# Loading q, k and v as nine consecutive tokens per partition, with the reordering done on the chip

## The chip, the cores and the metric

The kernel runs on one core of one Trainium2 chip. The time is the device time of one execution in microseconds (us), quoted as the median of several runs. Engines are named as in the profile: PE is the tensor engine (PEld its weight loads), DVE the Vector engine, ACT the Scalar engine, POOL is GpSimd (here it mostly issues loads), SP issues the stores. A ratio of two kernels is the mean time of one kernel's runs over that of the other's in the same rounds, so it is not quite the ratio of the medians that stand beside it. Executions over 1.5% slower than the fastest of the same kernel are left out of the means.

## The reference

Sliding-window causal attention (64 tokens back, batch 8, 8 heads, 576 tokens, head size 64), whose output is the input of a soft mixture of experts with 32 slots.

```python
def _attn_ref(q, k, v):                      # (8, 8, 576, 64)
    scores = scale * np.matmul(q, k.transpose(0, 1, 3, 2))
    mask = (rel >= 0) & (rel < 64)
    # ... softmax over the masked scores, then attn @ v

def _moe_ref(x, phi, w1, w2):                # x (4608, 512), 8 experts of 4 slots
    logits = x @ phi
    d = softmax(logits, over tokens); c = softmax(logits, over slots)   # shortened
    slot_input = (d.T @ x).reshape(8, 4, 512)
    for e in range(8):
        slot_out[e] = np.maximum(slot_input[e] @ w1[e], 0.0) @ w2[e]
    return c @ slot_out
```

The inputs are 28.3 MB of q, k, v and 33.5 MB of expert weights in fp32. The loads cast them to fp16, so 14.2 and 16.8 MB are written on the chip. The output is 9.4 MB.

## The kernel before

Each partition holds one token of a 128-token chunk, all heads beside each other. Every contiguous run in memory is one head's 64 numbers, 256 bytes. There are buffers for only five experts' weights, and `v_shf`, a copy of V moved by 64 tokens, is made by a transfer within the on-chip memory.

```python
for t_bf, t_dram in ((q_bf, q), (k_bf, k)):
    for c in range(NC):                                  # 5 chunks of tokens
        # ...
        nc.gpsimd.dma_start(out=t_bf[0:pn, c],
            in_=t_dram[b, :, 128 * c: 128 * c + pn, :].rearrange("h p d -> p h d"))
# ... the same for v_aug, then two transfers v_shf <- v_aug

def stage_tr(b, hp, q_bf, k_bf, small):                  # transposes: plain matmul with identity
    # ...
    for c in range(4):
        nc.tensor.matmul(tq[:, 128 * c:128 * c + 128], q_bf[:, c, h0:h0 + 2, :],
                         ident_h[:, :], start=True, stop=True)
    nc.scalar.copy(out=qT[:, 0:512], in_=tq[:, :])       # unit stride on both sides
    # ... k the same, its copy on DVE

    if b >= B - 5:
        load_expert(b - (B - 5))                         # five of the eight experts
```

The softmax here doesn't subtract the row's maximum and nothing guards it: scores larger than these inputs give would overflow.

## Time and profile before

The median was 295.81 us (293.19 to 296.01, 3 runs) before the prediction, and 294.73 us (4 runs) in the rounds of the comparison.

| stage, by the first matmul of the next | from, us | to, us | what bounds it |
|---|---|---|---|
| attention and the MoE's front | 0 | 216 | the 16 DMA queues, and waits for v_shf |
| experts | 216 | 260 | three experts' weights that come late |
| output | 260 | 291 | the stores |

From the page of the kernel before: its span, then the busy tenths of the DMA engines in 40 equal slices (7.3 us each), what they moved, and the sizes of the packets.

```profile
span 291.3 us, 5506 instructions
DMA  7999999999999999999999999900006999909997
GB/s 42 138 114 184 106 165 142 161 216 162 114 182 188 116 208 205 143 143 188 146 140 208 176 128 170 207 6 2 0 0 102 186 210 211 160 0 318 348 362 268
DMA packets 135338, 45.62 MB, mean 157 GB/s; under 512 B 113808, under 2 KB 126096, under 8 KB 135312
```

The engines read as busy in nearly every slice up to 190 us, but move 106 to 216 GB/s: most packets are small. Then they idle while GpSimd waits for a free weight buffer. From the list of waits of the kernel before (who waited for whom: us in total, times, longest):

```profile
POOL w1s L87 <- PE hj L276: 46.8, 2, 46.3
PE av L146 <- DMA v_shf<-v_aug: 37.8, 9, 9.1
```

The groups by line and shape give the durations (busy us, mean ns of one):

```profile
L112 DVE CAST kT<-tk 128x512 f16<-128x512 f32 x32 | 21.7, 679 | 13.2 <-PE tk L109 12.7
L106 ACT CAST qT<-tq 128x512 f16<-128x512 f32 x32 | 19.5, 610 | 9.3 <-PE tq L103 9.3
L127 DVE TENSOR_TENSOR pmt<-pmt,mask_95 128x256 f16<-128x256 f16 x64 | 18.5, 289 | 13.0 <-ACT pmt L126 12.2
```

A copy of 512 elements out of the matmul's result memory (PSUM) takes 0.61 us on ACT and 0.68 us on DVE.

### The profile page before, as it was taken

The page shows a single profiled execution, that of the slowest core. Times are in us where ns is not written, and L with a number is a line of the kernel's source. Part 1 is how long each engine was busy: PE and PEld are TensorE (multiplying, and loading weights), DVE is VectorE, ACT ScalarE, POOL GpSimd, SP SyncE. Part 2 cuts the span into 40 slices and gives each one's busy share as a digit, 9 for nine tenths or more (in the row PEclk, how much of TensorE's full clock was granted, in tenths as well). Part 3 has the DMA queues.
Part 4 walks back from the last instruction along what each step waited for, and adds up shares of the span by engine and source line. Part 5 has one row for each costly group of instructions (what it writes and reads, how often), then busy time and mean ns, then how long its engine had stood idle before and what let it go on. Part 6 is the DMA issues. An engine that isn't in the chain of part 4 may idle for free.

```text
span 291.3 us, 5506 instructions
## 1 busy us (share of the span) xinstructions
PE 200.2 (69%) x2080; PEld 114.1 (39%) x2080; DVE 126.2 (43%) x459; ACT 123.7 (42%) x403; POOL 116.1 (40%) x148
## 2 busy tenths in 40 slices
PE   0231858757983974996786598598878996685850
PEld 0120745544562552654454456354433432221100
DVE  1030871971682594378189068357320000023331
ACT  1030555553463653635465345464502332144552
POOL 9999396255486471838636380000003300000000
PEclk9999999955555885555596555575669999596555
DMA  7999999999999999999999999900006999909997
GB/s 42 138 114 184 106 165 142 161 216 162 114 182 188 116 208 205 143 143 188 146 140 208 176 128 170 207 6 2 0 0 102 186 210 211 160 0 318 348 362 268
DMA packets 135338, 45.62 MB, mean 157 GB/s; under 512 B 113808, under 2 KB 126096, under 8 KB 135312
## 3 DMA queue, kind: packets, MB, share of 16 engines
q0 software_dynamic: 125584, 30.97, 145.4%
q1 hardware_dynamic: 9728, 14.31, 16.5%
q8 instruction: 16, 0.26, 0.4%
q14 instruction: 10, 0.08, 0.1%
HBM read 61.93 MB, written 9.44 MB: 245 GB/s over the span
## 4 chain that ended last, share of the span: by engine, by line
DMA 29%; PE 22%; issue 20%; POOL 12%; DVE 7%; ACT 7%; ACTq 0%; DVEq 0%; SPq 0%; POOLq 0%
DMA v_shf<-v_aug 14%; DMA w1s<-in_moe_w_dram 7%; DMA out_dram<-ob 5%; POOL v_aug L219 4%; PE tx L164 4%; DMA v_aug<-in_v_dram 3%; PE av L146 3%; PE ltA L173 3%; POOL k_bf L212 3%; POOL q_bf L212 3%; ACT ob L303 3%; PE sA L122 2%; PE dps L198 2%; DVE kT L112 2%; ACT pmt L128 1%
## 5 line engine op out<-in xcount | busy, mean ns | idle before, releaser
L146 PE MATMUL av<-v_shf,pmt 128*64 128x65 f16 x320 | 30.9, 239 | 41.1 <-DMA v_shf<-v_aug 37.8
L212 POOL DMA_DIRECT2D q_bf<-in_q_dram x40 | 33.7, 873 | 32.1 <-PE tq L103 15.2
L126 ACT ACTIVATE pmt<-sA 128x256 f16<-128x256 f32 x64 | 24.8, 388 | 48.9 <-PE small L122 37.9
L212 POOL DMA_DIRECT2D k_bf<-in_k_dram x40 | 34.0, 874 | 21.2 <-DMA w2s<-in_moe_w_dram 12.4
L146 PEld LDWEIGHTS <-pmt 128*64 128x64 f16 x576 | 22.3, 140 | 50.3 <-issue 30.4
L219 POOL DMA_DIRECT2D v_aug<-in_v_dram x40 | 33.7, 871 | 8.0 <-DMA k_bf<-in_k_dram 2.6
L122 PEld LDWEIGHTS <-kT 64*128 64x128 f16 x576 | 23.6, 113 | 22.6 <-issue 10.8
L167 ACT CAST xT<-tx 128x512 f16<-128x512 f32 x32 | 18.1, 591 | 31.6 <-PE tx L164 31.6
L122 PE MATMUL sA<-qT,kT 64*128 64x64 f16 x512 | 25.9, 223 | 6.5 <-DVE kT L112 6.5
L146 PE MATMUL av<-v_aug,pmt 128*64 128x65 f16 x256 | 29.2, 241 | 0.0
L151 DVE RECIPROCAL rc<-av 128x5 f32<-128x5 f32 x64 | 9.6, 176 | 44.5 <-PE av L148 44.1
L152 DVE TENSOR_TENSOR x_b<-av,rc 128x320 f16<-128x320 f32 x64 | 28.2, 479 | 0.1
L112 DVE CAST kT<-tk 128x512 f16<-128x512 f32 x32 | 21.7, 679 | 13.2 <-PE tk L109 12.7
L128 ACT ACTIVATE pmt<-sA 128x256 f16<-128x256 f32 x64 | 25.0, 390 | 0.0
L87 POOL DMA_DIRECT2D w1s<-in_moe_w_dram x8 | 6.1, 768 | 47.1 <-PE hj L276 46.8
L306 DVE TENSOR_SCALAR ob<-cps,crcp 128x512 f32<-128x512 f32 x16 | 11.2, 745 | 29.9 <-PE cps L301 17.9
L127 DVE TENSOR_TENSOR pmt<-pmt,mask_95 128x256 f16<-128x256 f16 x64 | 18.5, 289 | 13.0 <-ACT pmt L126 12.2
L109 PE MATMUL tk<-ident_h,k_bf 128*128 128x128 f16 x128 | 22.5, 281 | 2.1 <-DMA k_bf<-in_k_dram 2.1
L276 PE MATMUL hj<-w1s,slot_inT 128*4 128x512 f16 x64 | 19.8, 428 | 5.9 <-DMA w1s<-in_moe_w_dram 5.5
L106 ACT CAST qT<-tq 128x512 f16<-128x512 f32 x32 | 19.5, 610 | 9.3 <-PE tq L103 9.3
L130 DVE TENSOR_TENSOR pmt<-pmt,mask_95 128x320 f16<-128x320 f16 x64 | 20.7, 323 | 3.6 <-ACT qT L105 0.3
L301 PE MATMUL cps<-slot_oa,dnumT 32*128 32x512 f16 (+1 forms) x40 | 15.9, 508 | 7.4 <-ACT ob L303 6.7
(72 smaller groups left out, 345.9 us busy)
## 6 DMA issues: line engine op xcount, KB each, us to landing
w1s<-in_moe_w_dram POOLq DMA_DIRECT2D x8, 1024.0 KB, 12.6
w2s<-in_moe_w_dram POOLq DMA_DIRECT2D x8, 1024.0 KB, 17.0
out_dram<-ob SPq DMA_DIRECT2D x8, 1024.0 KB, 4.5
q_bf<-in_q_dram POOLq DMA_DIRECT2D x32, 128.0 KB, 6.8
k_bf<-in_k_dram POOLq DMA_DIRECT2D x32, 128.0 KB, 8.0
v_aug<-in_v_dram POOLq DMA_DIRECT2D x32, 128.0 KB, 8.3
v_shf<-v_aug SPq DMA_DIRECT2D x8, 330.0 KB, 6.7
v_shf<-v_aug SPq DMA_DIRECT2D x8, 264.0 KB, 8.2
```

What stands on the lines that cost most here:

```text
L106: nc.scalar.copy(out=qT[:, 0:512], in_=tq[:, :])
L109: nc.tensor.matmul(tk[:, 128 * c:128 * c + 128], k_bf[:, c, h0:h0 + 2, :], ident_h[:, :], start=True, stop=True)
L112: nc.vector.tensor_copy(out=kT[:, 64:576], in_=tk[:, :])
L122: nc.tensor.matmul(dst, kT[r0:r0 + 64, 64 * i: 64 * i + 128], qT[r0:r0 + 64, 64 * i: 64 * i + 64], start=True, stop=True)
L126: nc.scalar.activation(pmt[:, 0:4, :], sA[:, 0:4, :], AF.Exp, scale=scale)
L128: nc.scalar.activation(pmt[:, 4:8, :], sA[:, 4:8, :], AF.Exp, scale=scale)
L130: nc.vector.tensor_tensor(out=pmt[:, 4:9, :], in0=pmt[:, 4:9, :], in1=mask_bB, op=ALU.mult)
L146: nc.tensor.matmul(av[r0b: r0b + 64, 65 * (i // 2): 65 * (i // 2) + 65], pmt[:, i, :], rhs, start=True, stop=True)
L152: nc.vector.tensor_tensor(out=x_b[:, 0:NC, 64 * h: 64 * h + 64], in0=avv[:, 0:NC, 1:65], in1=rc[:, 0:NC].unsqueeze(2).broadcast_to([128, N ...
L212: nc.gpsimd.dma_start(out=t_bf[0:pn, c], in_=t_dram[b, :, 128 * c: 128 * c + pn, :].rearrange("h p d -> p h d"))
L219: nc.gpsimd.dma_start(out=v_aug[0:pn, :, c, 1:65], in_=v[b, :, 128 * c: 128 * c + pn, :].rearrange("h p d -> p h d"))
L276: nc.tensor.matmul(hj[0:SPE, :], slot_inT[:, dc, SPE * e: SPE * e + SPE], w1s[:, dc, 512 * j: 512 * j + 512], start=(dc == 0), stop=(dc == ...
```

## The change

The intent is large runs and no second trip. One partition gets nine consecutive tokens of one head, 2304 contiguous bytes. After the transposes on PE the tokens stand in the wrong order (all tokens 0, 9, 18, ... first), and the copy out of PSUM puts them right by writing at a stride of nine elements. v_shf disappears; V is transposed a second time into windows instead. All weights are loaded during attention, and the expert and output stages use all of PE's columns. Work proceeds in 16 half batches of four heads.

```diff
-                nc.gpsimd.dma_start(
-                    out=t_bf[0:pn, c],
-                    in_=t_dram[b, :, 128 * c: 128 * c + pn, :].rearrange("h p d -> p h d"))
+            t = pld.tile([128, 2, S], FP16, name=nm, tag=nm)
+            nc.gpsimd.dma_start(
+                out=t,
+                in_=src[b, 4 * half:4 * half + 4].rearrange(
+                    "(x h) (g t) d -> (h g) x (t d)", x=2, h=2, t=T))      # T = 9
...
+    def t1(src, dst, on_vector):
+        for t0, n in ((0, 5), (5, 4)):
+            tr = ps.tile([128, 8, 128], FP16, name="tr", tag="tr")         # two buffers in all
+            for j in range(n):
+                for x in range(2):
+                    nc.tensor.transpose(tr[64 * x:64 * x + 64, j, :],
+                                        src[:, x, 64 * (t0 + j):64 * (t0 + j) + 64], ident[:, :])
+            o = dst.rearrange("p h (g t) -> p t h g", t=T)[:, t0:t0 + n]
+            i = tr[:, 0:n, :].rearrange("p t (h g) -> p t h g", h=2)
+            if on_vector:
+                nc.vector.tensor_copy(out=o, in_=i)
+            else:
+                nc.scalar.copy(out=o, in_=i)
...
+    def issue_loads(u):
+        if u + 2 < nu:
+            load_unit(u + 2)
+        for _ in range(1 if u >= 1 else 0):
+            if w_order and len(w_order) > 3:
+                f, e = w_order.pop(0)                                       # one w1 or w2
+                f(e)
```

The `tr` buffers serve the first transposes of q, k, v, the second of V, and all of the MoE front.

## The prediction

> **What bounds it now.** Span 291.3 us. The table by windows shows three stages. (1) 0–210 us, attention with the MoE front: the DMA row reads 9 in nearly every slice until 185 us, at only 140–185 GB/s of bytes written; of 135,338 packets 113,808 are under 512 B (q, k, v in 64-token runs), and v_shf, an SBUF copy that each batch waits for, stands in the chain of waits with 14%. PE is busy 75–80%. (2) 210–259 us, experts: only five experts' weights fit; GpSimd's next weight load waits 46.3 us for PE's hj, DMA is idle 190–220 us, then three experts (6.3 MB) arrive in 30 us, at 207 GB/s. (3) 259–291 us, output, 9.4 MB at 310–360 GB/s.
>
> **What the change does.** q, k, v: 2304 B contiguous per descriptor, 48 loads instead of 120, no v_shf (4.75 MB). All weights load during attention. In return 3 q/k/v reorder passes per half batch: per half batch ("unit", 16 of them) about 174 matmuls, in total 3,030 against 2,080.
>
> Costs per unit, estimates from the trace's durations:
> - DMA: 14.2+16.8 MB at 207 GB/s = 150 us in all; 0.885 MB of q/k/v is 4.3 us, a weight 5.1 us. In GpSimd's order the 16th unit's loads come after nearly all weights: six middle units carry two weights each, 14.4 us per unit; the last four carry none. The eleventh-to-twelfth unit arrives near 132 us.
> - PE: 128-column matmuls start 107 ns apart at clock 0.5, 56 ns at 1.0; 64-column ones in pairs about 55 ns a pair. At half clock 2.9 us first transposes, 1.9 us V transposes, 2.2 us QK/AV, 2 us MoE: 9.1 us. The Trainium skill, "TensorE: Matmul & The Clock Gate", Part 4, says transpose mode does not count as busy for the clock; before used plain matmuls, so its trace cannot tell. I expect mostly 0.5 here.
> - DVE: mask 2.1, V copies 2.0, k 1.5, normalise 2.3, MoE 1.2: 9.1 us, taking 0.53 ns per element (as the mask shows) for 16-bit PSUM copies with unit step; the skill, "VectorE: DVE Perf Modes", perf-mode tier table, allows up to 2x there. Otherwise 11.
> - ACT 5.4 us.
>
> With waits between the in-order engines (two shared transpose banks, one AV buffer) I take 10.5–12 us per unit where compute binds.
>
> **Sum.** To 132 us the DMA binds; then 5.3 units × 11 us = 58 and 8 us for the last batch's MoE: attention ends near 198. Experts, no weight waits, 22 us (PE, four column groups at once, near clock 1.0): 220. Output 31: 251, and 3 more outside the profile's span: **254 us**, range **236 to 274**. Faster by over 2%: 0.94; within 2%: 0.04; slower: 0.02. So about 40 us: some 27 from the expert stage, 12 from attention, 1–2 from output.
>
> **What would show it.** Right: no v_shf, few packets under 512 B, DMA about 200 GB/s until about 150 us and idle after; PE and DVE dense (over 85%) from 135 to 195 at clock about 0.5; experts under 26 us without DMA waits; output DMA-bound near 350 GB/s. Wrong: DMA below 180 GB/s in attention (2304 B runs not efficient); DVE's V copy of 512 elements near 0.68 us instead of 0.41; experts at clock 0.5 (34 us).
>
> **What would make it wrong.** Waits between PE, ACT and DVE making a unit 14 us or more, so that compute binds all 16 units (over 280); or full clock and short waits (8 us per unit), giving about 236.

## The result

The changed kernel takes 416.17 us (median, 415.28 to 416.71, 4 runs) against 294.73 us: a ratio of 1.4104 (95% interval 1.4025 to 1.4184). It is 41% slower, where 254 us was expected. The result is correct.

The page of the changed kernel (slices of 10.4 us):

```profile
span 414.8 us, 6919 instructions
PE 208.4 (50%) x3028; PEld 152.7 (37%) x3028; DVE 204.5 (49%) x420; ACT 221.8 (53%) x160; POOL 51.7 (12%) x77
DMA  8993997969693979596423324240003300000798
GB/s 110 191 180 49 137 153 105 184 84 184 89 187 48 188 124 177 89 173 112 58 28 43 46 30 57 30 54 5 1 2 53 50 2 2 2 0 2 287 377 246
DMA packets 31069, 40.83 MB, mean 98 GB/s; under 512 B 1856, under 2 KB 22336, under 8 KB 31040
```

What the change was meant to do to the DMA, it did: 31,069 packets instead of 135,338, and hardly any below 512 bytes. But no engine is busy for more than 53% of the span, and the DMA is idle for nearly half of it. Attention ends at 361 us (before: 216). The experts then take 23 us (before: 44) and the output 31 (before: 32).

Groups by line and shape of the changed kernel:

```profile
L143 ACT COPY qT<-tr 128x640 f16<-128x640 f16 x16 | 47.5, 2971 | 15.2 <-PE tr L136 15.2
L143 ACT COPY qT<-tr 128x512 f16<-128x512 f16 x16 | 40.0, 2497 | 0.0
L141 DVE COPY kT_111<-tr 128x512 f16<-128x512 f16 x8 | 20.9, 2616 | 0.0
L169 DVE COPY vw_113<-tr 128x512 f16<-128x512 f16 x32 | 12.2, 417 | 30.0 <-PE tr L167 30.0
L191 DVE TENSOR_TENSOR pm<-pm,mask_98 128x512 f16<-128x512 f16 x64 | 24.4, 418 | 15.7 <-ACT pm L187 15.6
```

The copies after the first transposes (lines 141 and 143) take 2.5 to 3.0 us on both engines. The copy of V into windows (line 169) has the same 512 fp16 elements from the same PSUM buffers on the same engine and takes 0.417 us. The one difference in plain sight is where the elements are written. Three such pairs of copies stand in every half batch: 5.2 us for k on DVE and 10.6 us for q and v on ACT ((85.5 + 42.0 + 41.9) / 16, from the page's rows of line 143).

What follows from that shows in the order of time. From the timeline of the changed kernel (start us, us, what, and in brackets how long the engine had been idle and what ended it):

```profile
156.52 1.01 PE L167 MATMUL tr<-ident,vT_103 128*128 128x128 f16 x8 [1.24 <-ACT qT L143]
158.58 5.21 DVE L141 COPY kT_111<-tr 128x640 f16<-128x640 f16 x2 [0.25 <-PE tr L136]
161.59 1.01 PE L249 MATMUL tr<-ident,x_bp 128*128 128x128 f16 x8 [2.52 <-DVE kT_111 L141]
163.84 0.37 PE L167 MATMUL tr<-ident,vT_103 128*128 128x128 f16 x2 [1.24 <-DVE rc L220]
165.57 5.23 ACT L143 COPY vT_112<-tr 128x640 f16<-128x640 f16 x2 [6.45 <-PE tr L136]
170.86 1.03 PE L167 MATMUL tr<-ident,vT_112 128*128 128x128 f16 x8 [3.72 <-ACT vT_112 L143]
```

A pair of copies (the two that empty one tensor's transposes) holds both `tr` buffers, and PE, whose next work in order is a transpose into one of them, stands still (2.5 and 3.7 us here). So the slow copies on the two engines do not overlap with each other but follow one another. GpSimd's next load waits for PE in turn. From the waits:

```profile
POOL qn L61 <- PE tr L136: 74.7, 12, 8.9
POOL vn L61 <- PE av L214: 70.7, 11, 8.6
PE tr L167 <- ACT qT L143: 25.5, 15, 2.1
PE tr L167 <- ACT vT_112 L143: 20.8, 8, 3.7
```

A half batch takes 21.9 us: the first transposes of v run from 13.2 us (half batch 0) to 342.3 us (half batch 15), which is 329.1 / 15.

### The profile page after: what moved, and what is told of

The parts are those of the page before. It is cut to its first block, busy times and chain, and to the rows that moved or that the text cites. A ratio compares the mean times of both kernels' runs of the same rounds, so it can differ in the third digit from the quotient of the medians.

```text
span 414.8 us, 6919 instructions
## 1 busy us (share of the span) xinstructions
PE 208.4 (50%) x3028; PEld 152.7 (37%) x3028; DVE 204.5 (49%) x420; ACT 221.8 (53%) x160; POOL 51.7 (12%) x77
## 2 busy tenths in 40 slices
DMA packets 31069, 40.83 MB, mean 98 GB/s; under 512 B 1856, under 2 KB 22336, under 8 KB 31040
## 5 line engine op out<-in xcount | busy, mean ns | idle before, releaser
L143 ACT COPY qT<-tr 128x640 f16<-128x640 f16 (+1 forms) x32 | 85.5, 2734 | 15.2 <-PE tr L136 15.2
L143 ACT COPY vT_112<-tr 128x640 f16<-128x640 f16 (+1 forms) x16 | 42.0, 2845 | 52.4 <-PE tr L136 52.4
L143 ACT COPY vT_103<-tr 128x640 f16<-128x640 f16 (+1 forms) x16 | 41.9, 2832 | 44.5 <-PE tr L136 44.5
L187 ACT ACTIVATE pm<-sc 128x1024 f16<-128x1024 f32 (+1 forms) x48 | 46.4, 967 | 33.0 <-issue 28.1
L141 DVE COPY kT_102<-tr 128x640 f16<-128x640 f16 (+1 forms) x16 | 41.7, 2794 | 9.9 <-PE tr L136 9.9
L141 DVE COPY kT_111<-tr 128x640 f16<-128x640 f16 (+1 forms) x16 | 41.7, 2790 | 2.2 <-PE tr L136 2.2
L167 PE MATMUL tr<-ident,vT_112 128*128 128x128 f16 x144 | 19.4, 307 | 45.6 <-ACT vT_112 L143 20.8
L169 DVE COPY vw_104<-tr 128x512 f16<-128x512 f16 (+1 forms) x48 | 15.0, 353 | 47.9 <-PE tr L167 47.9
L167 PE MATMUL tr<-ident,vT_103 128*128 128x128 f16 x144 | 19.9, 306 | 37.1 <-ACT vT_103 L143 13.4
L191 DVE TENSOR_TENSOR pm<-pm,mask_98 128x512 f16<-128x512 f16 (+1 forms) x96 | 29.8, 349 | 15.7 <-ACT pm L187 15.6
L167 PEld LDWEIGHTS <-vT_112 128*128 128x128 f16 x144 | 14.4, 135 | 48.0 <-issue 25.0
L169 DVE COPY vw_113<-tr 128x512 f16<-128x512 f16 (+1 forms) x48 | 15.2, 352 | 30.0 <-PE tr L167 30.0
L214 PEld LDWEIGHTS <-pm 128*64 128x64 f16 x576 | 28.1, 158 | 4.7 <-issue 2.4
L167 PEld LDWEIGHTS <-vT_103 128*128 128x128 f16 x144 | 14.8, 137 | 40.8 <-issue 25.5
L136 PE MATMUL tr<-ident,vn 128*64 128x128 f16 x288 | 22.2, 311 | 10.6 <-DVE kT_102 L141 2.4
## 6 DMA issues: line engine op xcount, KB each, us to landing
w1s<-in_moe_w_dram POOLq DMA_DIRECT2D x8, 1024.0 KB, 10.5
w2s<-in_moe_w_dram POOLq DMA_DIRECT2D x7, 1024.0 KB, 10.6
```

Of the source, the lines that this page charges most:

```text
L136: nc.tensor.transpose(tr[64 * x:64 * x + 64, j, :], src[:, x, 64 * (t0 + j):64 * (t0 + j) + 64], ident[:, :])
L141: nc.vector.tensor_copy(out=o, in_=i)
L143: nc.scalar.copy(out=o, in_=i)
L167: nc.tensor.transpose(tr[:, h * n + w, :], st["vT"][:, h, 64 * i:64 * i + 128], ident[:, :])
L169: nc.vector.tensor_copy(out=st["vw"][:, wins[0]:wins[0] + n, h::2, 0:64], in_=tr[:, h * n:h * n + n, :].rearrange("p w (x d) -> p w x d", ...
L187: nc.scalar.activation(pm[:, :, 0:2 * n, :], sc[:, :, 0:128 * n].rearrange("p x (w q) -> p x w q", q=64), AF.Exp, scale=scale)
```

## The experiments

The theory (A): a 2-byte element written 18 bytes after the one before is slow, whichever engine writes it; the shared buffers then multiply the loss. Rivals: (B) the copies are slow because of what runs beside them in the full kernel; (C) reading fp16 from PSUM by a pattern of several dimensions is slow; (D) the copies are not the point, the two buffers and a tensor engine at half clock would cost as much anyway. Of the eight runs, m1_copies and e1_dense are wrong; the other six are correct.

### m1_copies: the copies alone

Only copies of one filled PSUM buffer (or of on-chip memory, SBUF) into SBUF, three of each kind, first all on DVE and then all on ACT, with nothing beside them. It was executed once, so its state is unknown.

```diff
+        for s in (1, 2, 3, 4, 5, 6, 7, 8, 9, 10, 12, 16, 18, 32):
+            dd = d.rearrange("p a b -> p (a b)")[:, 0:512 * s].rearrange("p (a b) -> p a b", b=s)
+            cp(eng, dd[:, :, 0], flat16[:, 0:512])          # three times, on each engine
+        # and the kernel's own copy ("orig"), and with its loops swapped ("swap"):
+        o = dst.rearrange("p h (g t) -> p h g t", t=9)[:, :, :, 0:n]
+        i = p16[:, 0:n, :].rearrange("p t (h g) -> p h g t", h=2)
```

> Wrong result on purpose: only copies and transposes, to time them one by one. Theory A (a 2-byte write that lands 18 bytes after the one before is slow, whatever engine writes it): 512 elements from PSUM take about 0.4 to 0.7 us at element strides 1 to 4, rise between 4 and 8, and take 2.4 to 2.8 us at stride 8, 9 and above, on the Vector and the Scalar engine alike; from SBUF to stride 9 as slow; the kernel's own copy of 640 near 2.9 us here too, with nothing beside it. With the loops swapped (runs of 5 or 4 written together, PSUM read at a stride) below 1.2 us. Theory B (the copy is slow because DMA writes, the tensor engine and both copying engines load the same memory in the full kernel): the kernel's own copy takes under 1 us here, where nothing runs beside it. Theory C (fp16 in PSUM read by a three-dimensional pattern is slow): stride 9 in one dimension is fast, the kernel's own form slow, the swapped form slow too.

Groups of m1_copies on DVE; the names W..b, c, e, i, j mean stride 1, 2, 4, 8, 9, G.. is an fp32 destination, K.. the kernel's own copy:

```profile
L42 DVE COPY Wvxbas<-psh 128x512 f16<-128x512 f16 x3 | 1.0, 394 | 0.0
L42 DVE COPY Wvxcas<-psh 128x512 f16<-128x512 f16 x3 | 1.9, 709 | 0.0
L42 DVE COPY Wvxeas<-psh 128x512 f16<-128x512 f16 x3 | 3.5, 1304 | 0.0
L42 DVE COPY Wvxias<-psh 128x512 f16<-128x512 f16 x3 | 7.1, 2612 | 0.0
L42 DVE COPY Wvxjas<-psh 128x512 f16<-128x512 f16 x3 | 7.1, 2592 | 0.0
L42 DVE CAST Gvtwo<-psh 128x512 f32<-128x512 f16 x3 | 1.9, 674 | 0.0
L42 DVE CAST Gvnine<-psh 128x512 f32<-128x512 f16 x3 | 2.9, 1054 | 0.0
L42 DVE COPY Kvorigfive<-psh 128x640 f16<-128x640 f16 x3 | 8.5, 3079 | 0.0
L42 DVE COPY Kvswapfive<-psh 128x640 f16<-128x640 f16 x3 | 2.5, 874 | 0.0
```

| destination stride, fp16 elements | 1 | 2 | 3 | 4 | 5 | 6 | 7 | 8 | 9 | 16 | 32 |
|---|---|---|---|---|---|---|---|---|---|---|---|
| DVE, ns for 512 | 394 | 709 | 989 | 1304 | 1631 | 1958 | 2285 | 2612 | 2592 | 2483 | 2575 |
| ACT, ns for 512 | 594 | 771 | 1120 | 1460 | 1804 | 2147 | 2490 | 2831 | 2816 | 2703 | 2796 |

From stride 3 the time rises by a nearly constant 0.3 us per step and stops rising at stride 8, that is at 16 bytes. 2612 / 512 is 5.1 ns for each element that falls into a 16-byte line of its own; at stride 4, where two elements share a line, the 256 lines cost 1304 / 256 = 5.1 ns each as well. So for these copies of 2-byte elements out of PSUM the time goes with the lines touched, not with the elements. The kernel's own copy takes 3.08 us with nothing beside it: rival B falls. A stride of nine in one dimension is as slow as the kernel's three-dimensional form, and the swapped form, which has the same number of dimensions and reads PSUM at a 256-byte stride, takes 0.87 us: rival C falls. My expectation that strides up to 4 would be cheap was wrong: the cost begins at once.

The Trainium skill, "Advanced Engine Details and Errata", section "Memory Cachelines", says that SBUF has 16-byte lines, that it takes at least two hits on a line to absorb the latency, and that a different line for each access costs time. The limit at 16 bytes agrees. For 4-byte elements "two hits" agrees too (674 ns at stride 2, 1054 at stride 9). For 2-byte elements it does not: two hits per line (stride 4) take 1304 ns, against 709 at stride 2.

One thing stays open: I expected the copy from SBUF to be as slow, but there DVE writes at stride 9 in 1427 ns, while ACT needs 2801 ns. No run here says why DVE then pays half.

### e1_dense: the same copies, densely written

Wrong: the tokens stay in transposed order. Nothing else changes.

```diff
-            o = dst.rearrange("p h (g t) -> p t h g", t=T)[:, t0:t0 + n]
+            o = dst.rearrange("p h (t g) -> p t h g", t=T)[:, t0:t0 + n]
```

> Wrong result on purpose: the same copies out of the first transposes, same sizes, same engines, but written densely (tokens left in transposed order). Theory A: 640 elements fall from 2.97 us to 0.4-0.8 us, a half batch from 21 us to 10-13 us, the whole from 416 to 240-270 us, as the prediction summed it. Theory D (not the copies but the two shared transpose banks, the single AV buffer and the tensor engine at half clock set 21 us): the copies get fast, but the whole stays above 330 us.

It took 237.31 us (236.95 to 237.7), a ratio to the kernel before of 0.7983 (0.7936 to 0.803). From the groups (640 and 512 together, mean ns):

```profile
L143 ACT COPY vT<-tr 128x640 f16<-128x640 f16 (+1 forms) x32 | 19.3, 643 | 32.4 <-PE tr L136 32.2
L141 DVE COPY kT<-tr 128x640 f16<-128x640 f16 (+1 forms) x32 | 14.1, 452 | 15.0 <-PE tr L136 14.9
```

179 of the 416 us go with the way of writing alone (416.17 - 237.31). Rival D falls: the buffers, the number of instructions (6919) and the order of the program are as they were.

### e2_swap: a right result, with the loops of the copy swapped

```diff
-            o = dst.rearrange("p h (g t) -> p t h g", t=T)[:, t0:t0 + n]
-            i = tr[:, 0:n, :].rearrange("p t (h g) -> p t h g", h=2)
+            o = dst.rearrange("p h (g t) -> p h g t", t=T)[:, :, :, t0:t0 + n]
+            i = tr[:, 0:n, :].rearrange("p t (h g) -> p h g t", h=2)
```

> A right result: the copies iterate head, group, token instead of token, head, group, so that runs of 5 or 4 tokens are written together and PSUM is read at a stride of 256 bytes. Theory A with only writes dear: 640 elements in 0.7-1.2 us and a total of 245-275 us, near e1. If strided PSUM reads cost as much as strided writes: copies stay at 2.5-3 us and the total above 390 us.

245.71 us (244.97 to 245.95), ratio 0.8261 (0.8212 to 0.831), correct. The same elements go to the same places; only the order in which they are written differs, five or four neighbours together.

```profile
L143 ACT COPY qT<-tr 128x640 f16<-128x640 f16 x16 | 12.1, 757 | 12.0 <-PE tr L136 11.9
L141 DVE COPY kT<-tr 128x640 f16<-128x640 f16 x16 | 13.1, 820 | 7.8 <-PE tr L136 7.7
GB/s 88 147 191 208 209 207 209 208 208 213 205 212 206 210 208 208 211 207 211 206 209 209 206 206 158 1 3 98 79 3 0 3 0 4 0 264 378 379 373 155
```

With this the change is a gain, and the prediction's stages can be read from a profile: the DMA moves 208 GB/s and has most of its work done by about 150 us (slices of 6.1 us), then it idles; attention ends at 190.5 us, the experts take 22.4 us, the output 30.9.

### e3_banks: buffers of their own for the first transposes, copies left slow

```diff
-            tr = ps.tile([128, 8, 128], FP16, name="tr", tag="tr")
+            tr = ps.tile([128, 8, 128], FP16, name="tq", tag="tq", bufs=2)
...
-        sc = ps.tile([128, 2, 512], FP32, name="sc", tag="sc")
+        sc = ps.tile([128, 2, 512], FP32, name="sc", tag="sc", bufs=1)
```

> Right result: the first transposes get two PSUM banks of their own (taken from the score tile, which goes from two buffers to one), the copies stay slow. If the loss is mainly that the slow copies hold the two shared banks and everything queues behind them: 416 falls to 310-350 us (the Scalar engine then has 11 us of slow copies and 3 us of exp in each half batch, 14 us, as its floor). If the engines' copy time in sequence is what counts: 390-416 us.

357.54 us (357.2 to 358.15), ratio 1.2029 (1.1945 to 1.2113), between the two expectations and nearer the first. (The scores lost a buffer for it, and no run shows what that alone costs; the 59 us below are net of it.) Of the 170 us between the changed kernel (416) and e2_swap (246), some 59 come back when the slow copies no longer hold the buffers that everything else needs. This part is a wait that the copies cause, not copy time, and it would have been in no sum of busy times. The other 112 are not copy time alone either. PE still stands still until a slow copy frees one of the first transposes' two own buffers (now named `tq`), 71 us in all:

```profile
PE tq L136 <- DVE kT L141: 36.8, 16, 3.0
PE tq L136 <- ACT qT L143: 34.3, 25, 2.6
```

No run splits these 112 us into the copies' own time and such waits.

### e4_pinned: e2_swap with the weights spread evenly

The scheduler of the build had moved weight loads ahead, because they wait for nothing: six middle half batches carried two weight tensors each, the last four none. Here GpSimd's loads stay in program order.

```diff
-            nc.gpsimd.dma_start(out=t, in_=...)
+            tc.keep_in_program_order(nc.gpsimd.dma_start(out=t, in_=...))
...
-        nc.gpsimd.dma_start(out=w1_t[e], in_=...)                # and w2
+        tc.keep_in_program_order(nc.gpsimd.dma_start(out=w1_t[e], in_=...))
```

> A right result: the swapped copies, and GpSimd's loads held in program order, one weight tensor behind each half batch of q, k, v from the second on (the scheduler had put two weights into each of six middle half batches and none into the last four). If my account of the weights' order is right (DMA-bound to about 125 us, then 60 us of computing with idle DMA): the DMA stays near 208 GB/s to the end of attention, the last q, k, v land near 135 us, attention ends at 160-168 us instead of 190, the total is 215-225 us. If instead computing (11 us or more in each half batch) binds all the way, the order is worth nothing: 240-248 us.

216.59 us (214.6 to 218.3; the run of 218.3 counts as slow and is not in the ratio), ratio 0.727 (0.7181 to 0.7359), correct: the order of the loads is worth 29 us (each against the kernel before in its own rounds: 0.8261 and 0.727). Attention ends at 161.7 us. The DMA (slices of 5.4 us) now has no hole before the experts, and DVE is busy 87% of a stretch in the middle. From the page, and from the table by windows (after the bounds and the length: busy us of PE, PEld, DVE, ACT, POOL with instruction counts, then granted clock, DMA share, GB/s):

```profile
GB/s 73 146 188 206 212 206 207 209 209 208 208 211 206 207 211 208 206 207 212 206 211 206 209 207 208 212 206 212 173 18 3 0 5 0 116 376 378 380 351 148
60.00:80.00 20.00, 15.82 (x384) 12.72 (x382) 17.48 (x50) 10.91 (x18) 6.18 (x9) 1.00 1.19 208
```

The changed kernel in a stretch of the same length, for comparison:

```profile
160.00:180.00 20.00, 9.28 (x151) 7.58 (x152) 9.73 (x22) 12.32 (x7) 3.16 (x5) 1.00 0.85 131
```

384 matmuls in 20 us against 151. (The clock of 1.00 in this last line is not a reading; see "Why the prediction was wrong".) A half batch takes 9.2 us (first v transposes from 9.1 to 147.1 us, over 15).

### e5_runs: 256-byte runs again

As e4_pinned, but q, k, v go into tiles with 66 places for every 64 elements, so that a descriptor can't be longer than one token's 256 bytes. There are two loads where there was one, and GpSimd is busy for 112.9 us instead of 51.7, so some of the difference may be GpSimd's.

```diff
-            t = pld.tile([128, 2, S], FP16, name=nm, tag=nm)
+            t = pld.tile([128, 2, T, 66], FP16, name=nm, tag=nm)
+            for x in range(2):
+                ... out=t[:, x, :, 0:64], in_=src[...].rearrange("(x h) (g t) d -> x (h g) t d", ...)[x]
```

> A right result: as e4_pinned, but q, k, v land in a padded tile (66 elements for each 64), so that every descriptor carries 256 bytes as before the change, in place of 2304; twice the number of load instructions. If run length is what the nine-token layout buys: q, k, v move at about 100 GB/s instead of 208, the DMA needs 210-220 us, the total is 270-290 us. If the 16 queues keep up with small runs when nothing else is in the way: below 230 us.

238.2 us (237.38 to 239.53), ratio 0.8058 (0.7985 to 0.8131), correct. My figure of 100 GB/s was far too low, and 238 falls between the two expectations. The long runs are worth at most about 22 us here, not 60:

```profile
GB/s 44 112 94 152 150 183 167 194 164 203 159 198 168 191 177 179 186 173 192 165 198 165 195 167 193 175 181 185 208 212 178 22 0 4 0 321 378 377 373 155
DMA packets 130141, 40.84 MB, mean 173 GB/s; under 512 B 113216, under 2 KB 121408, under 8 KB 130112
```

The Trainium skill, "DMA: Bandwidth & Descriptors", section "Specifications", gives 512 bytes as the smallest transfer at line rate. That agrees in direction: 150 to 200 GB/s where 256-byte runs and weights mix, 208 without them.

### e6_wlate: all weights behind the last q, k, v

```diff
-        for _ in range(1 if u >= 1 else 0):
+        for _ in range(0):
```

> A right result: as e4_pinned, but all 16 weight tensors are queued behind the last q, k, v. If computing alone takes 9-10 us per half batch: attention ends near 160 us; the weights need 81 us from about 130 us on, the experts end near 215 us, the total is 245-255 us, the same as with the scheduler's order (245.7), so that loading weights during attention in that order was worth nothing. If computing needs 11 us or more: attention ends at 185 us or later, total above 255 us.

240.66 us (239.87 to 241.13), ratio 0.8134 (0.8077 to 0.819), correct. Attention ends at 160.4 us, so computing alone takes 9.1 us per half batch (first v transposes from 9.6 to 145.8 us, over 15). The experts then wait for weights and end at 207.0 us:

```profile
GB/s 86 154 185 208 205 118 103 102 102 102 102 103 101 98 107 97 95 110 87 95 159 186 209 207 212 209 209 211 207 213 206 211 211 207 64 305 379 377 372 152
```

The attention stage could be fed at about 100 GB/s. Against this kernel, loading weights during attention gains 24 us when they are spread evenly (e4_pinned), and loses some 4 or 5 in the order that the change was built with (e2_swap, in other rounds).

### e7_pinbanks: e4_pinned with the buffers of e3_banks

The two edits of e3_banks on top of e4_pinned.

> A right result: as e4_pinned, and the first transposes have two PSUM banks of their own, scores one buffer instead of two. If the shared banks still hold things up when the copies are short: 3-10 us faster than e4_pinned. If the second score buffer is worth more: slower by 3-15 us.

216.16 us (214.04 to 216.21), ratio 0.7291 (0.7221 to 0.7361), correct. The intervals of e4_pinned and e7_pinbanks overlap almost wholly, so neither expectation was met. With short copies the two edits together change nothing that these runs can show; a gain from the own buffers and a loss from the single score buffer could still cancel, which was not tested. Both are the fastest versions, 27% below the kernel before.

## Why the prediction was wrong

The step that failed is two terms of the sum, "k 1.5" in the line on DVE and the copies of q and v within "ACT 5.4 us". They were priced as if they wrote densely: 1152 elements at the 0.68 us per 512 of the kernel before are 1.5 us. The k copies took 5.2 us per half batch. The prediction doesn't split its 5.4 us on ACT; at 0.61 us per 512 the 2304 elements of q and v would be 2.7 us (an estimate from the kernel before), and they took 10.6, twice the whole of ACT's line. The diff shows the stride of nine, and the skill's section on lines was there to be read; the prediction used neither. m1_copies shows the cost alone, e1_dense and e2_swap show that it is the whole miss, its consequences (the waits and the lower clock) included.

Point by point:

- *"Waits between PE, ACT and DVE making a unit 14 us or more"* was named as the danger, and it came: 21.9 us per half batch. The cause is the copies; e3_banks gives 59 us of the loss to their hold on the shared buffers.
- *Attention to 198 us, experts 22, output 31.* In the changed kernel 361, 23 and 31. In e2_swap, where only the order of the copies' elements differs, 190.5, 22.4 and 30.9: 245.7 us against the predicted 254, within the range. So the rest of the sum came close, though its 11 us per half batch was too long and its clock too low (below).
- *DMA: 207 GB/s, weights bunched in the middle, DMA idle at the end.* Right where the copies are quick (208 GB/s in e2_swap); e4_pinned shows that the bunching cost 29 us. In the changed kernel the DMA mostly waited, at 98 GB/s on average.
- *10.5 to 12 us per half batch where compute binds.* Too much: 9.1 us in e6_wlate. The allowance for waits was not needed.
- *V's copy 0.41 us.* Right: 0.417 us. The skill's "VectorE: DVE Perf Modes", perf-mode tier table (up to twice the rate from PSUM), agrees, for a copy that writes densely.
- *Clock mostly 0.5.* Right for the changed kernel, not for the reason given. Eight transposes of 128 columns take 1.01 us there, of which the last is 0.31: (1.01 - 0.31) / 7 is 0.10 us from start to start. The 1.00 that the table by windows prints for this stretch is not a reading: the packed trace holds no clock record before 356 us, and the table counts time without a record as full clock. In e2_swap the same eight take 0.61 us:

```profile
44.13 0.61 PE L167 MATMUL tr<-ident,vT 128*128 128x128 f16 x8 [0.20 <-ACT qT L143]
```

With 0.22 us for the last, that is 56 ns from start to start. In the kernel before, the plain 128-column matmuls start 56 ns apart between 50 and 59 us, where the clock on record is 1.00, and 107 ns apart between 60 and 96 us, where it is 0.50. So transposes can run at full clock when they stand among other matmuls, against the skill's "TensorE: Matmul & The Clock Gate", Part 4, which says that the fast clock doesn't engage for them. Whether transposes alone would bring it about was not tested. The half clock of the changed kernel came with the slow copies: e1_dense and e2_swap, which change only those copies, reach the pace of 56 ns at 23 and 34 us. No run separates what the half clock cost from what the waits cost.

## What to carry to other kernels

Before pricing a copy, look at the distance between the elements it writes one after another, not only at their number: the same copy took 3.0 us or 0.8 us by the order of its loops alone. When a slow step holds a buffer that other steps share, its cost is its own time plus the time for which everything behind that buffer stands still. After a change that moves loads, read the order in which they are really issued; here one load per half batch instead of two in the middle was worth 29 us, more than the 22 us, at most, of the long runs.

## What the Trainium skill lacked or had wrong

- "Advanced Engine Details and Errata", section "Memory Cachelines", has no size for the cost, and its "two hits on a line" doesn't hold for 2-byte elements copied from PSUM: about 5.1 ns for every 16-byte line touched, on DVE and (5.5 ns) on ACT, from stride 3 on. For 4-byte elements in lines of their own it was 2.1 ns on DVE (1054 / 512).
- No page that I read says that reading PSUM at a wide stride is cheap for a copy. The swapped copy, which reads at a stride of 256 bytes, took 874 ns for 640 elements on DVE, against 3079 ns for the kernel's own form.
- "TensorE: Matmul & The Clock Gate", Part 4: transposes among other matmuls ran 56 ns apart, the pace of full clock, in e2_swap.
- The same page, "Seeing it yourself", warns that clock records in a trace can't be trusted fully. It doesn't say what was seen here: no clock record at all before 356 us in the changed kernel, so that a table printed 1.00 while transposes started 0.10 us apart.
- "DMA: Bandwidth & Descriptors": no figure for a mix of 256-byte and long runs; it was 150 to 200 GB/s here (e5_runs), against 208 for long runs alone.
